# Forgetting attention and SwiGLU in one kernel: queries and keys of batch 0 loaded as two pairs of 256 tokens, with the written order redone

## Chip, cores and metric

The kernel runs on 1 core of one Trainium2 chip. The metric is device time in microseconds (us) of one execution; shorter is better.

## What is computed

The reference takes q, k, v of shape (8 batches, 8 heads, 576 tokens, 64) and a forget gate f, and feeds the attention's output, as 4608 rows of 512, to a SwiGLU layer of width 1536:

```
scores = scale * q @ k^T + (cum[:, None] - cum[None, :])     # cum = cumsum(log f), causal
attn   = softmax(scores);   x = attn @ v
xn     = x / sqrt(mean(x*x) + 1e-6) * rms_g
out    = (silu(xn @ w_gate) * (xn @ w_val)) @ w_out
```

## The kernel before, in words

Tokens of a batch are cut into five pieces j = 0 to 4 (four of 128 tokens, one of 64). For each batch, q and k are loaded from memory with a cast from float32 to bfloat16 by DMAs that POOL issues; each piece is turned so that the head dimension lies on the partitions; scores of a piece of queries against one piece of keys are one tile (8 small matmuls, `score_block`, L510); ACT takes the exponential (L552); POOL masks the diagonal tile (L560); PE multiplies with the scaled values (`values`, L566, matmuls in L581); DVE divides (L600, L604); `norm` (L613) makes the normalised rows, which PE turns for batches 0 and 1 (L651) and the DMA engines turn for the others. From there `gate` (L828) multiplies with w_gate and w_val (L838), and `project` (L877) with w_out (L916). The last token groups use a scheme with seven products for eight (`seven`, L746, matmuls in L773).

How a piece of q or k is loaded and turned:

- `load_qk` (L334) loads one piece of 128 tokens: one DMA for q and one for k (issued at L340). In memory one token of one head is a run of 256 bytes.
- `load_qk2` (L345) loads 256 tokens in one DMA (issued at L352). Partition p holds tokens 2p and 2p+1, so that one run is 512 bytes. Its buffers are four places of the tile `wt`, which is needed for weights only later; in the trace these DMAs and matmuls therefore carry the name `wt`.
- `turn_pe` (L448) turns a piece on PE for batches 0 and 1: 4 transposes for a single piece (L458), 16 for a pair (L464). One copy each then takes the turned q (DVE) and k (ACT) out of PSUM into QT and KT (L476).
- `PAIRS` (L16) says which pieces begin a pair. Before, batch 0 has a single piece 0, a pair of pieces 1 and 2, and a single piece 3 (loop at L413); batch 1 has two pairs.

The work is not ordered by a scheduler at run time. Every instruction group is a unit, made in a fixed order of creation by `P.add`; `Plan.run` (L125) then sorts the units by a written rank: each two letters of `ORDER` (L34) are the rank of one unit, in base 62, in order of creation. `SLOTS` (L75) gives in the same way the buffer that each use of a ring takes. Each engine works through its own units strictly in this order, and waits where an operand or a buffer is not there yet. PE has two score buffers (`sc`), so that a block of two score tiles needs the exponentials of the two tiles before it to be done. POOL's order holds its DMA issues, its masks and small steps of `norm`, one behind the other; SP issues the other DMAs. `load_w` (L369) loads thirds of w_gate and w_val (called wg0, wv0, wg1 and so on below).

Of the kernel before, what the change touches and what calls it, by code (L numbers as in the profile page):

```python
# [31 lines left out]
WEIGH_ACT = "gv"  # L32
LETTERS = string.digits + string.ascii_letters
ORDER = (  # L34
    "0302000105060y0C0g0b0h040l0i0m0p0q0z0c0d0F0M0K07080e0f090a0n0o0j0k0w0x0O0P0t0u0D0E0r0s14151p1q1y1z1U"
    "1V2f2g38392K2L3T3U0H0I0R0S1e1f1J1K18190Y0Z2y2z2V2W32333v3w2q2r3P3Q3H3I4a4b4w4x4B4C5j5k3A3B4f4g5X5Y4o"
    "4p4S4T5S5T4J4K6r6s71724Z506G6H7o7p6v6w7e7f8u8v6l6m6Q6R9s9t7G7H6A6B8j8k7L7M8e8f9M9N9q9r9Y9Za0a1ayazaN"
    "aO9w9x9D9E9Q9Rb4b5apaqaDaEbMbNbcbdcAcBbHbIcQcRc6c7egehcGcHcLcMf0f1bubvdsdtg4g5dfdgcZd0gagbdXdYezeAfo"
    "fpeFeGe3e4dhdidKdLg7g8hWhXesetfAfBgEgFgPgQgVgWiqirhbhchKhLhdheinioiQiRhshtjpjqiBiCkLkMh1h2iwixgJgKkl"
    "kmkgkhlhlikqkrkAkBkPkQlElFlllmmkml0v0A0B0G0N0J0Q0W0U0V0L0T17121a161k1u1h1m1o1r1v1E0X1b1d1g111B1H1N1S"  # L40
    "221Y231j1n1s1A252x2M272c2k2m24281F1Q3t2t2A2P2G2S2Y343r413i3s3m3z4n3Z443J3K4t4u3o4G5i5a4k4l4E4F6f5s5z"
    "5D5H5Q6b686c5w5x5o5p6g624P4Q5E5F786i6x6M6t5c5d5L5M7y6E6O6X6K747n7k7s63646S6T7T7x7I7B7S827Z8476777h7i"
    "8P8c8z8r7C7D7N7O9k8M8X8Z94969d7X7Y898a9U9h9p9l9L8n8o7t7uaI9C9H9O8T8U9A9Bbo9Wacaia8araHaLa6a7avawaSb2"
    "b8bhbfbUc2bXcdaXaYbrbsa9cbaeafamanbAcicncucvbabbbjbkdncDcPd6cKcWdpdcdRcEcFd2d3cUdGdPdWe6eledeNdvdwdI"
    "dJfveCePeKdkdle0e1gddHeWfbfNeZfHcycze8e9gwfiftfGgjf9fadSdTgIfUg3fXeHeIgegffZghgngpgogyh0gTfQfRglgmfS"
    "h9hjhBhghGi2icihejekhEhFjhhVhOhPgrgsjMipiEj4iyi0i1i6i7jGiLj3jyiSj9jgjmjTiuivieifhSjzjNjFjXksk0k8jCjD"
    "jKjLijkCkKkHk3k4kbkclNjnkTkYl1l0lWiYiZjVjWlzlblAlIm0kUkVkEkFmylOlYlTl9lalolpm9mamjmqmfmumDmImdmemEmF"
    "nkmPmTnsmWn7ncnand101i131c1w1x1D1G1M1R1T1Z2a2e2j2n2C2E2U36353a3c3f3L3S4h4q4M4W4Y5e5V656n6u6W6Z797g7m"
    "7v7A7F7R7V81888m8A8t8y9c9ia2a5ajatauaAaCaMb6bgbibnbGbLbRbVcJcOcVcYd1d5dqdAdNdQeqeyeJeOeYfff8fdgcgigq"
    "gugxgCgNgSgXgZhihlhyhAi8idiAiIjejljvjEjOjQjYk2k7kekkkpkzkIkWlcl7lfm6mimcmhmmmomrmCmzmHmJmNmVmYnJnNnX"  # L50
    "o3o7og1l1t1C1I1O1L1P1W1X21262b2i2o2w2u2F2R2Z31aTdzlnm4m53d3j3n3W4L4V3y3V405K5C5P61676d6j6I6L9b9yf7hw"
    "hx8g8b8l8W9f9g8E8J8K8w8C8G8R90918O9899bEeoeSeUeVb0aRb3bKbPbQblbybzbObZc3ccckclc9cfcgfLiJmpmvmwdEecee"
    "erewexeDfgfhfjfmfrfxfCfDfzfJfKhTjck5l3l4gHhphvhCiFiGhNiNiOikiXj1j6jajbj8jjjkkRltoqqYqZkokjkwl6lUlVld"
    "lwlxlglrlJn2n5n6m8mLmMmAmGojonoomtmZnznSoJoKpcpJpKo1oSoYp8pzpApmprpspupyqiqQqR202l292h2s2d2v2p2B2H2D"
    "2N2J2Q2X3k3E3q3x3N3D3M3R585W484z662I3p2O2T3C3u423F3X49303e3b3h3l373Y3g3G46434U4D4N534X4i5545524e4j57"
    "4c4y4v4A4H4r4R4I4O543O4m474d4s6C6o5q6h737a6V6F5b6a5n5r6p5A6e5R5Z6k7r7W7Q80836Y8B7d7l8H5u6z5O6N7b5g5G"
    "5t5y5J7c7E7w7z7P7K877U8d8i8q8L8I8Q958S97939e9o6P7j70757q8h8F8p8s8Nc0cec5cacj9Sa49Xaaad9Pab9T9VahaPaW"
    "aVb7beagaGalaoaKbmbJbtbBbScmcNcrcwcTakbqasaBbxbwbWbDbFc1c4cpchcocCbCc8bTbYcqaxaUaFaQaZfEg6fPg2ggcSde"
    "cXd7dof3flfefkfFdyebdMeaeieneMeveLf6d8dVdjdre2fMgYfVfYh4fcfIfqfyfOd4dmd9dddxeffseBeEfwgRhfh5h7hmdudO"
    "dBdFe5ibitiiiDiKgLh3gOgUh8iHj2iMiTj7h6hIhahhiahkhrhohqhDhnilhHi5izhzhYhMhRi4jBjPjJjUk6iPjoj0jdjAj5k1"  # L60
    "jujHkaigjiimisjrgtgDgzgGgMkvmUn0nGljlHocn8nwlCmQngmOnqnvnxnFnEnCnInQnRnUo6nZnAnOofomnTo4obovoioyoCoF"
    "nKnWo8oIoGoNoeoDn1ntnlnrnDk9lkkfktlvmKnhn4nbnukdkNkxkSl2mSnMnpnyo0lelKlulBlPlslSlDlLlZlGmnm3mbmxnLo9"
    "ounBpgpjptpCpnpEpMpPpRpWpTqbpBpYpXq1q8q9qcqhqoquqkqCpFqeqwqFqgqmqvqynHnPosoznVokotoMoOoVoQp4oaohoHp0"
    "olopoLp7oRp3papbnYorpfpioXpGpqpNo2o5oBp2odoAoEp9p1plpopppdpkpHpSpwpvpOqPpUq0r1q4oPpDpIq7pQr5pVq3qlqt"
    "r4qpqxqBqAqDqEqKqOqTr2rdqWrorerprsrvrwrzrDrRrJrSrVs0qSrOrys4rirZsgslq6qfqGqJqqqIqUqVr3rjr7rtqNr0qXrk"
    "r6rarfrqrmrFrurPqsrgrUrYrLs2rEs8rGrQs7serWs3s6sjsbsisusms5s9sascshsdsnsfsCsKsqsTsksxsLsWsOsSsFsXrxrA"
    "rKrIrTspsAsDsrstswsHszsGt2t6sEsMsNsUsQt0tht3tqtAtktIsItbt9tNtctnsRtEt8titytBtvtttxtYunusu1uKtMtXtStZ"
    "uhu4u7u6uputubuItPukuMuQuaueuuuwsYt1tdtgtatjtptltztFtstWtotuu2u5tGtOtTugu0u8uiudtmtJufumu3ulucuq515B"
    "5m7J595N5h6y565f5l5v9m9n5I5U60696q6D9J9K6J6U85868x8Dcsct8V9a929v8Y9z9Ga3dadb9u9F9j9IaJb1f4f5b9bpdCdD"
    "cxcIjsjtdUepemfndZe7eueRg0g1eTeXeQf2fufTgAgBgkgvjRjSfWg9iViWhuhUhJkihQhZi3i9jwjxiUjfjIjZknkym1m2kGkO"  # L70
    "owoxkukJnnnokDkXl5lqkZl8lylMlQlRlXm7mgmsmBmRninjmXn3nenfn9nmoToUoZp6peqaoWp5phpxuDuEpLq2pZq5qdqnr8r9"
    "qrqzrbrcqjqHqLqMrlrCrrsyrhrnrBrHrMrNrXs1sosssvsBtQtRsVsZt4t5sJsPtUtVt7tetwtDtftrtCtHtKtLujuouruxu9uy"
    "uBuCuGuVuXuYuzuJuNuOuAuFuHuTuvuPuUv0v3v4v1v2uLuSuRuWuZv6v9vavhvivbvlvpvqvnvovmvtvwvxvuvvv5v8vfvgvcvd"
    "v7vevjvkvrvs")
SLOTS = (  # L75
    "751b7a6362435110692802330754611170531262234023077651332432705b415542030169201a3302681541266b20177132"
    "2014533279005a6532661701135841742b721169332872410a23133054512665001739727a00200b42516118624543301b17"
    "71260040183951042a633112223573007b576333221173001561043122201100167312010541110321076100101454210733"
    "1011601200461031045720101103775012610544301702070101354106121015470017210034110611070104132015456013"
    "6100232017101455410630720011241100713104560011601234710070150277155011443103601200201571041750163132"  # L80
    "0101244100751104542016110324110701060053043233321311301053041033210111005004211241051100150340532013"
    "5310011221152001320353033202132013312230214131322301201202006220311303000143015262410033052722315103"
    "5261610735230212317213710230012635070323111010023111111000033110311200012110300131022003000032112100"
    "2201100120113110321031112300301010002101113003011020020102210220031010101011133102110101001311301103"
    "1102010311010122002100211001013200230113310131121103001211133012101200112100210020002171654506371011"
    "0103211330113002201331011012110026174342511114721231650015433657002001265345146210057101423570136474"
    "7252111003105406640115412730640007213167565012100433222217616210003112431260112012333003166262100310"
    "00004522412001200020465002100141510131034120020751351457312030266221127301205346576122415734323406")
# [981 lines left out]
```

## Time and profile before

| | us |
|---|---|
| median of 3 runs | 352.58 |
| lowest and highest run | 352.28, 355.83 |
| the profiled execution's own time | 351.74 |
| its span in the profile | 350.0 |

The span runs from the first to the last event that the profiler records; 1.74 us of the profiled execution lie around it. "Busy" is the time in which an engine has an instruction under way. Busy time of PE (TensorE's matmuls) includes the time until the last result of a group is out, so two groups that follow closely overlap a little in the listing. The DMA engines are a common resource of all queues.

### The profile page before, as it was taken

What the parts mean: (1) busy time and instruction counts of PE and PEld (TensorE: products, weight loads), DVE (VectorE), ACT (ScalarE), POOL (GpSimd) and SP (SyncE); (2) the same over time, 40 slices, a digit from 0 to 9 for tenths busy, and PEclk for the clock granted to TensorE, in tenths of its full rate; (3) what the DMA queues carried; (4) which work ended last, traced back from release to release, by engine and by line L of the source; (5) the groups of instructions that cost most, each with busy time, mean ns of one, the idle gap of its engine ahead of it and who ended that gap; (6) DMA issues with size and microseconds to landing.
All of it is one profiled execution on the core that took longest, in us unless ns stands there. A gap on an engine that the chain in (4) does not pass through costs nothing.

```text
span 350.0 us, 10530 instructions
## 1 busy us (share of the span) xinstructions
PE 333.9 (95%) x4289; PEld 259.9 (74%) x4314; DVE 275.3 (79%) x515; ACT 265.8 (76%) x440; POOL 204.5 (58%) x244
## 2 busy tenths in 40 slices
...
GB/s 128 215 217 233 200 153 137 155 149 117 182 136 162 162 157 147 198 140 165 182 174 122 180 168 139 166 84 121 3 85 45 2 76 62 2 30 36 59 90 153
DMA packets 159465, 44.89 MB, mean 128 GB/s; under 512 B 145012, under 2 KB 158840, under 8 KB 159416
## 3 DMA queue, kind: packets, MB, share of 16 engines
...
q14 instruction: 15, 0.12, 0.2%
...
## 4 chain that ended last, share of the span: by engine, by line
PE 87%; DVE 4%; ACT 2%; DMA 2%; issue 2%; POOL 1%; DVEq 0%; ACTq 0%; POOLq 0%
PE ff L838 31%; PE ff L916 19%; PE late L773 10%; PE ff L773 8%; PE sc L533 7%; PE ff L581 7%; PE late L916 4%; DMA qk<-in_q_dram 2%; ACT PT L552 1%; DVE ga L852 1%; PE ff L464 1%; POOL qk L340 1%; DVE KT L737 1%; POOL wt L352 0%; DVE x L604 0%
## 5 line engine op out<-in xcount | busy, mean ns | idle before, releaser
L552 ACT ACTIVATE PT<-sc 128x1024 bf16<-128x1024 f32 x96 | 94.7, 1023 | 20.0 <-PE sc L533 19.8
L838 PE MATMUL ff<-xT,wv 128*128 128x128 bf16 (+2 forms) x452 | 67.3, 289 | 1.6 <-DVE ga L852 1.1
L838 PE MATMUL ff<-xT,wg 128*128 128x128 bf16 (+2 forms) x451 | 67.5, 289 | 0.8
L845 DVE SCALAR_TENSOR_TENSOR hT<-ga,ff 128x512 bf16<-128x512 f32 x68 | 46.0, 684 | 14.3 <-PE ff L838 11.3
L824 POOL TENSOR_TENSOR hT<-PT,PT 128x512 bf16<-128x512 f32 x20 | 25.9, 1310 | 53.5 <-DVE PT L800 27.6
L852 DVE SCALAR_TENSOR_TENSOR ga<-th,ff 128x512 f32<-128x512 f32 x68 | 46.1, 682 | 9.2 <-ACT th L850 8.1
L850 ACT ACTIVATE th<-ff 128x512 f32<-128x512 f32 x68 | 40.0, 597 | 13.1 <-PE ff L838 7.9
L838 PEld LDWEIGHTS <-wv 128*128 128x128 bf16 x464 | 36.0, 98 | 18.2 <-issue 1.0
L838 PEld LDWEIGHTS <-wg 128*128 128x128 bf16 x464 | 35.9, 98 | 16.9 <-issue 0.2
L916 PEld LDWEIGHTS <-hT 128*128 128x128 bf16 x432 | 41.4, 98 | 6.8 <-issue 0.2
L560 POOL TENSOR_SCALAR_AFFINE_SELECT PT<-PT 128x1024 bf16<-128x1024 bf16 x32 | 36.6, 1147 | 12.3 <-ACT PT L552 12.2
L581 PEld LDWEIGHTS <-PT 128*128 128x128 bf16 (+1 forms) x896 | 32.0, 102 | 8.4 <-issue 1.6
L581 PE MATMUL ff<-Vs,PT 128*128 128x65 bf16 (+1 forms) x896 | 37.2, 196 | 0.0
L604 DVE TENSOR_TENSOR x<-ff,rden 128x256 f32<-128x256 f32 (+1 forms) x80 | 33.9, 424 | 3.2
L916 PE MATMUL ff<-wo,hT 128*128 128x256 bf16 x288 | 35.4, 273 | 0.0
L916 PEld LDWEIGHTS <-sm 128*128 128x128 bf16 x324 | 31.1, 98 | 5.3 <-issue 0.7
L493 POOL TENSOR_TENSOR Vs<-v,decT 128x512 bf16<-128x512 f32 (+1 forms) x30 | 31.6, 1055 | 5.3 <-DMA v<-in_v_dram 5.2
L533 PE MATMUL sc<-QT,KT 64*128 64x128 bf16 (+1 forms) x960 | 33.6, 215 | 0.5 <-ACT PT L552 0.3
L533 PEld LDWEIGHTS <-KT 64*128 64x128 bf16 x960 | 24.6, 97 | 12.2 <-issue 10.8
L926 DVE TENSOR_TENSOR ores<-ores,ff 128x512 f32<-128x512 f32 (+1 forms) x38 | 25.2, 663 | 8.6 <-PE ff L916 7.9
L340 POOL DMA_DIRECT2D qk<-in_q_dram x34 | 29.9, 881 | 1.0 <-POOLq L1054 0.8
L340 POOL DMA_DIRECT2D qk<-in_k_dram x34 | 29.7, 875 | 0.0
...
## 6 DMA issues: line engine op xcount, KB each, us to landing
out_dram<-ores SPq DMA_DIRECT2D x32, 256.0 KB, 2.6
v<-in_v_dram SPq DMA_DIRECT2D x25, 256.0 KB, 4.3
qk<-in_q_dram POOLq DMA_DIRECT2D x26, 128.0 KB, 5.7
qk<-in_k_dram POOLq DMA_DIRECT2D x26, 128.0 KB, 5.9
v<-in_v_dram POOLq DMA_DIRECT2D x7, 256.0 KB, 7.3
wg<-in_moe_w_gate_dram POOLq DMA_DIRECT2D x3, 512.0 KB, 8.7
wv<-in_moe_w_val_dram POOLq DMA_DIRECT2D x3, 512.0 KB, 9.4
...
```

Source lines behind the costliest of these rows:

```text
L340: nc.gpsimd.dma_start(out=T_qk[h.slot][0:n, :].rearrange("p (h d) -> p h d", d=D), in_=src[b, :, p0:p0 + n, :].rearrange("h p d -> p h d"))
L533: nc.tensor.matmul(t[:, par, c:c + n], lhsT=kt[r, p, kj * 128:(kj + 1) * 128], rhs=qt[r, p, qi * 128:qi * 128 + n], start=not x, stop=True ...
L552: nc.scalar.activation(T_of_p[hp.slot][:, 0:2 * half].rearrange("p (a c) -> p a c", a=2)[:, :, 0:cols], T_sc[h.slot][:, :, 0:cols], ACT.Ex ...
L560: nc.gpsimd.affine_select(out=d, in_=d, pattern=[[0, 8], [1, n]], compare_op=ALU.is_ge, fill=0.0, base=0, channel_multiplier=-1)
L581: nc.tensor.matmul(T_ff[hpo.slot][r0:r0 + n, p * 65:p * 65 + 65], lhsT=T_of_p[h.slot][:, c:c + n], rhs=vs[:, kj, 2 * p + par, :], start=(k ...
L604: nc.vector.tensor_tensor(d, po[r0:r0 + n, :, 0:D], bcast(r[r0:r0 + n, :], D), ALU.mult)
L773: nc.tensor.matmul(t[:, c * HTK:(c + 1) * HTK], lhsT=w[:, d, (2 * u + c) * 128:(2 * u + c + 1) * 128], rhs=r[:, d, :], start=(start and c ...
L838: nc.tensor.matmul(T_ff[h.slot][:, c:c + n], lhsT=w[:, dc, fc * 128:(fc + 1) * 128], rhs=xT[:, dc, t0:t0 + n], start=(dc == 0), stop=(dc = ...
L845: nc.vector.scalar_tensor_tensor(hT, in0=three[0], scalar=0.5, in1=three[1], op0=ALU.mult, op1=ALU.mult)
L850: th = act(0.6, key - 0.1, lambda: nc.scalar.activation(T_th[ht.slot], T_ff[hg.slot], ACT.Tanh, scale=0.5), [ug], take=[ht])
L852: a = dve(0.69, key - 0.1, lambda: nc.vector.scalar_tensor_tensor(T_ga[ha.slot], in0=T_th[ht.slot], scalar=1.0, in1=T_ff[hg.slot], op0=ALU ...
L916: nc.tensor.matmul(t[:, s * HD:(s + 1) * HD], lhsT=a()[:, fc, s * 128:(s + 1) * 128], rhs=w[:, fc, :], start=(not more and s == ss[0] and ...
```

## The change

q and k of pieces 0 to 3 of batch 0 come as two pairs (pieces 0 and 1, pieces 2 and 3) instead of a single piece, a pair and a single piece. The strings for the order and the slots are replaced as a whole.

```diff
-PAIRS = {(0, 1), (1, 0), (1, 2)}
+PAIRS = {(0, 0), (0, 2), (1, 0), (1, 2)}
...
 ORDER = (
-    "0302000105060y0C0g0b0h040l0i0m0p0q0z0c0d0F0M0K07080e0f090a0n0o0j0k0w0x0O0P0t0u0D0E0r0s14151p1q1y1z1U"
+    "0302000105060l0y0j0m04070p0g0k0q0r0z0c0d0H180N08090e0f0a0b0n0o0h0i0s0t0B0C0u0v191a0w0x1o1p1H1I2f2g2P"
...
 SLOTS = (
-    "751b7a6362435110692802330754611170531262234023077651332432705b415542030169201a3302681541266b20177132"
+    "751372636241503001231174166372620321504021597b331a08526526416731330379225042501b0a137754001873414661"
...
-    for at, (j, two) in ((-16, (0, False)), (-15, (1, True)), (-13, (3, False))):
+    for at, (j, two) in ((-16, (0, True)), (-13, (2, True))):
         (load_qk2 if two else load_qk)(0, j, at)
         for i in range(j, j + 1 + two):
             load_v(0, i, at + 0.01)
```

There are 1956 units before and 1948 after: two loads fewer are made (an issue and a landing each) and two turns fewer (the transposes and their copy each). Read against the order of creation, the two `ORDER` strings begin like this on the engines. Here "q0" is q of piece 0, "q01" the pair of pieces 0 and 1, "b1" stands for batch 1, S(q,k) is a score tile of batch 0, V(q) the products with the values, "mask" POOL's mask of the diagonal tile of that query piece, T(j) the transposes of normalised piece j, G(j) the first products of `gate` for piece j:

```
POOL before  q0 k0 k12 q12 v3 q3 v1 k3 b1q01 v2 b1k01 mask0 b1k23 wg0 b1q23 b1v0 mask1 wv0 norm0 wg1 mask2 ...
POOL after   q01 k01 q23 v1 k23 v3 wv0 v2 b1q01 b1k01 b1q23 mask0 b1k23 mask1 wg0 b1v1 norm0 wg1 mask2 ...

PE before    turn q0, turn k0, decay, S(0,0), turn k12, turn q12, turn q3, V(0), S(1,0..1), V(0), turn k3,
             S(2,0..1), turn b1q01, S(2,2), turn b1k01, V(1), S(3,0..1), V(1), turn b1k23, T(0), V(2), S(3,2..3),
             V(2), T(1), G(0), turn b1q23, S(b1), V(3), ...
PE after     turn q01, turn k01, decay, S(0,0), turn q23, S(1,0..1), turn k23, V(0), V(0), S(2,0..1), V(1), V(1),
             S(2,2), S(3,0..1), turn b1q01, turn b1k01, S(3,2..3), V(2), T(0), V(2), T(1), turn b1k23, turn b1q23,
             S(b1), G(0), V(3), ...

ACT before   copy k0, exp(0,0), copy k12, exp(1,*) x2, copy k3, exp(2,*) x3, copy b1k01, exp(3,*) x2, copy b1k23, ...
ACT after    copy k01, exp(0,0), exp(1,*) x2, copy k23, exp(2,*) x3, exp(3,*) x2, copy b1k01, exp(3,*) x2, ...
```

Further on the same units come in another interleaving all the way; the end of PE's order (the products of the last group and four halves) is alike.

## Rows read from the trace of the kernel before

**Rows 1.** The page, part 1: busy time, share of the span, instructions

```profile
PE 333.9 (95%) x4289; PEld 259.9 (74%) x4314; DVE 275.3 (79%) x515; ACT 265.8 (76%) x440; POOL 204.5 (58%) x244
```

**Rows 2.** Busy by stretch: length, PE, PEld, DVE, ACT, POOL, granted clock, DMA share, GB/s

```profile
0.00:24.34 24.34, 15.81 (x239) 12.22 (x240) 19.18 (x53) 17.44 (x20) 21.65 (x30) 1.00 1.43 185
24.34:50.00 25.66, 25.47 (x516) 24.23 (x514) 24.11 (x47) 24.54 (x40) 20.10 (x29) 1.00 1.31 198
...
215.00:230.00 15.00, 13.78 (x188) 9.23 (x191) 13.47 (x21) 12.85 (x22) 10.60 (x12) 1.00 1.33 166
...
340.00:350.00 10.00, 5.09 (x46) 4.16 (x43) 3.60 (x8) 0.59 (x1) 0.00 (x0) 0.93 0.46 133
```

**Rows 3.** Timeline of PE: start, duration, instruction, idle before it

```profile
12.07 0.61 PE L458 MATMUL ff<-ident,qk 128*128 128x128 bf16 x4 [0.73 <-DMA qk<-in_q_dram]
...
15.89 0.61 PE L533 MATMUL sc<-QT,KT 64*128 64x128 bf16 x8 [0.30 <-ACT PT L552]
...
17.97 1.07 PE L464 MATMUL ff<-ident,wt 128*64 128x128 bf16 x16
...
19.52 1.04 PE L533 MATMUL sc<-QT,KT 64*128 64x128 bf16 x16
...
21.02 0.64 PE L464 MATMUL ff<-ident,wt 128*64 128x128 bf16 x16
...
24.34 1.06 PE L838 MATMUL ff<-xT,wg 128*128 128x128 bf16 x16
25.32 0.64 PE L464 MATMUL ff<-ident,wt 128*64 128x128 bf16 x16
...
26.45 0.66 PE L581 MATMUL ff<-Vs,PT 128*128 128x65 bf16 x16
...
226.90 0.81 PE L838 MATMUL ff<-xT,wv 128*128 128x512 bf16 x3 [1.07 <-DVE ga L852]
```

**Rows 4.** Timeline of ACT, copies and exponentials of the start

```profile
10.36 1.31 ACT L476 COPY KT<-ff 128x1024 bf16<-128x1024 bf16 x1
13.90 1.94 ACT L552 ACTIVATE PT<-sc 128x1024 bf16<-128x1024 f32 x2 [2.23 <-PE sc L533]
15.73 0.59 ACT L476 COPY KT<-ff 128x512 bf16<-128x512 bf16 x1
```

**Rows 5.** Timeline of POOL: issues of q0, k12, b1k23, wg0, b1q23, wv0; one mask

```profile
1.31 1.10 POOL L340 DMA_DIRECT2D qk<-in_q_dram  x1 [0.81 <-POOLq L1054]
...
3.29 0.90 POOL L352 DMA_DIRECT2D wt<-in_k_dram  x1
...
11.21 1.20 POOL L560 TENSOR_SCALAR_AFFINE_SELECT PT<-PT 128x1024 bf16<-128x1024 bf16 x1
12.26 0.99 POOL L352 DMA_DIRECT2D wt<-in_k_dram  x1
13.16 0.85 POOL L373 DMA_DIRECT2D wg<-in_moe_w_gate_dram  x1
13.90 0.99 POOL L352 DMA_DIRECT2D wt<-in_q_dram  x1
...
16.70 0.88 POOL L373 DMA_DIRECT2D wv<-in_moe_w_val_dram  x1
```

**Rows 6.** The same six issues, one each: KB written, us from issue to landing

```profile
qk<-in_q_dram POOLq DMA_DIRECT2D x1, 128.0 KB, 4.3
wt<-in_k_dram POOLq DMA_DIRECT2D x1, 256.0 KB, 5.4
wt<-in_k_dram POOLq DMA_DIRECT2D x1, 256.0 KB, 6.4
wg<-in_moe_w_gate_dram POOLq DMA_DIRECT2D x1, 512.0 KB, 8.6
wt<-in_q_dram POOLq DMA_DIRECT2D x1, 256.0 KB, 9.3
wv<-in_moe_w_val_dram POOLq DMA_DIRECT2D x1, 512.0 KB, 9.7
```

More of the change, by code (lines that the diff above doesn't have):

```diff
@@ L34 @@
 ORDER = (
-    "0302000105060y0C0g0b0h040l0i0m0p0q0z0c0d0F0M0K07080e0f090a0n0o0j0k0w0x0O0P0t0u0D0E0r0s14151p1q1y1z1U"
[L36 to L74, printed above, removed]
-SLOTS = (
-    "751b7a6362435110692802330754611170531262234023077651332432705b415542030169201a3302681541266b20177132"
[L77 to L88, printed above, removed]
@@ new lines @@
+    "0302000105060l0y0j0m04070p0g0k0q0r0z0c0d0H180N08090e0f0a0b0n0o0h0i0s0t0B0C0u0v191a0w0x1o1p1H1I2f2g2P"
+    "2Q1X1Y35360E0F0J0K1A1B1g1h0R0S0Y0Z2C2D292a2Y2Z2l2m494a2U2V3j3k4L4M3Q3R3K3L54553C3D4Z505R5S4d4e5f5g63"
+    "6457584R4S5K5L5z5A6j6k7b7c7k7l3Z406W6X6M6N7E7F6s6t797a7J7K9i9j7A7B8u8v9J9K8m8na9aa9V9W9A9Ba5a67W7X9F"
+    "9Gadaeapaqb0b1aVaWaLaMb6b7cPcQcsctdidjdYdZcNcObubvcucvd8d9cCcDaNaOcIcJd0d1evewdPdQdCdDfhfigegfdddefN"
+    "fOgBgCfxfyf7f8f3f4g5g6dRdSfYfZgvgwhdheh8h9ieifiYiZioipgXgYi8i9iHiIhyhzhjhkjKjLi2i3hKhLjxjyktkukokpkJ"
@@ new lines @@
+    "kKkykzkfkglBlClGlHljlkmUmV0A0D0G0I0L0M0P0V0Q0U110X140O0T0W151t161i1d1k1n1s1m1r1v1z1E1Q1K1R1u1x1w1D2y"
+    "2p231W2d2s271T1Z1P1U472o2u2J2z2G2N2T3c3q333p3O41484w4D3H3I3T3U5M4W535c42434l4m5Q5o5q5t5G5U61676b4T4U"
+    "4y4z6n6h4H4I5u5v736f6v6D6q5a5b5V5W7q6F6P6V6Z7d7o7j7u68695C5D6Q7y7L7P7U8b80876x6y71728e8q8y8O81826H6I"
+    "8S928W93969a9g7h7i8i8j9U9k9r9q9O898a9o9pa19H9Na38I8J9Q9RaAagamatarazaFaP9y9zaDaEaHb2b5babcbjbBbobAav"
+    "awaRaS9m9xaiajbYbZbFbTc3c9cfbQbRbKbLcgcFcLdpcYdadodhdKcyczdkdld6dBe2dJe9epeeekdHdIeOePfdeFeMfcdwdxd2"
@@ new lines @@
+    "d3eIeSfkfpfrfvfHezeAdUdVfBfFfJfPfWemenfTfUgbg1gcgseteugRgSh4gDgJgMgVh7hlhtgjgkh0h1iShQhThYhZi7ihimiO"
+    "g3g4fLfMfSgrgFgGgtguhFisizj5iPhphqiuiviFj1jljIj8jtjBjwjCiUiVjrjskPjJjUjOk3kck7kIjDjEjQjRl2klkAkvjajb"
+    "k0k1kCkkkLl4lqkTlsk8k9j2j3kWl8lplflWkRkSldlem0lKlYlQlllmlulvmsm3mdmjm8mkmqmumemflTlUnbmEmWn0mKn1n9n6"
+    "nk101712131b1f1e1j1G1L1M1V222c2h2k2F2M3237383e3f3m4i4o4B4F4Q4X51596c6g6B6K6R6Y74777r7v7M7Q7Z858d8k8o"
+    "8r8x8A9d9D9u9P9E9LaoauayaBaCaIb4bebwbCbGbJbNbXcmcxcUcXdLdTdXe7e3e6edeqeEeHeLeUfAfGg7gdgggigngEgAgIhm"
```

36 lines of the change are left out of this document (added).

## The prediction

> **What bounds the kernel now.** I read the page's busy shares first, then busy time by stretch, then the timelines of PE, ACT and POOL in the start, and last the landings of single DMAs. PE is busy for 333.91 of 350.0 us [rows 1, 2], so only 16.1 us can be won by better cover. The stretches say where they lie: 24.34 - 15.81 = 8.53 us before the first product of `gate`, 0.19 us from there to 50, 1.22 us between 215 and 230, and 10 - 5.09 = 4.91 us in the last 10 us, where the last results are added and stored [rows 2]. The other stretches share 16.1 - 14.85 = 1.24 us. From 24.34 us on PE has next to no gap, so whatever the change does to the moment at which PE is first kept full comes out at the end one for one, and that is where I look. The tail has the same last products and I take it as unchanged.
>
> The moment must be compared for equal work. After the change PE's order puts turn b1q23 and a score block S(b1) ahead of G(0); before, they come behind it. Before, G(0), the turn and the block are all done at 26.45, and G(0) itself takes 25.32 - 24.34 = 0.98 [rows 3]. So "as early as before" means for the new order: G(0) starts at 26.45 - 0.98 = 25.47.
>
> **The change, part by part.** *Work of PE, DVE, ACT, POOL.* Four turns of a single piece go, two turns of a pair come. A single turn's row is 0.61 us, but the next group starts 0.40 later; a pair's is 1.07 [rows 3]. That is 2 x 1.07 - 4 x 0.40 = +0.54 at most and 2 x 1.07 - 4 x 0.61 = -0.30 at least. I don't add it separately: the chain below holds every turn. ACT copies two pairs instead of two singles and a pair: 1.31 - 2 x 0.59 = +0.13 [rows 4]; it stands in the chain too. POOL makes two issues fewer, some 0.9 each [rows 5], -1.8 us, and gains nothing by it while the DMA queue is the slower part, as the next point shows.
>
> *The first landings.* Counting float32 as it is read, q0, k0 and k12 are 256 + 256 + 512 KB, and k12 lands at 3.29 + 5.4 = 8.69 [rows 5, 6]. The new q01 and k01 are the same 1024 KB, issued at the same first places, so k01 lands at 8.69 by that row. By the pace of the following stretch it could be earlier: from 8.69 to the landing of b1k23 at 12.26 + 6.4 = 18.66 come 3328 KB, 0.77 us per 256 KB, against 3.08/3 = 1.03 between q0 (1.31 + 4.3 = 5.61) and k12; with 0.77 it is 5.61 + 3 x 0.77 = 7.9. I take 8.4, near the row of the same transfers.
>
> *The score chain.* From k01: turn 1.07 (9.5), copy of the pair on ACT 1.31 (10.8), the block S(0,0) of 8 matmuls 0.61 (11.4), its exponential 1.94/2 = 0.97 (12.4). Meanwhile turn q23 (11.4 to 12.4), then S(1,0..1), 1.04 (13.5), two exponentials 1.94 (15.4), copy k23 1.31 (16.7), three exponentials of piece 2 (19.6). Only then is the second score buffer free for S(3,0..1), which ends at about 20.0. Before, the same block ended at 19.52 + 0.97 = 20.49 [rows 3, 4]. On scores the new order is thus 0.5 us ahead. But PE's fillers are gone from that stretch: before, three of the four turns of batch 1 lay between these blocks or right behind, after, all four come behind S(3,0..1).
>
> *From there to G(0).* Left at 20.0 are 4 turns of pairs, 2 score blocks, V(2) twice (12 matmuls each), T(0) and T(1). PE shows two paces for the same form: 16 transposes take 1.07 at 17.97 and 0.64 at 21.02 [rows 3], though the granted clock reads 1.00 (2.4 GHz) in the whole stretch [rows 2]. By net times (start to start) of the quick pace, 0.57 a turn, 0.55 a block, 0.46 and 0.3 the others, the list is 4 x 0.57 + 2 x 0.55 + 2 x 0.46 + 2 x 0.3 = 4.9 us, 24.9, and some 0.3 more since S(3,2..3) waits for two exponentials: 25.2. (0.46 and 0.3 are estimates, by the ratio of the matmul counts to the block's 16.) By the slow pace each is about 1.8 times that, 8.7 us: 28.7.
>
> *The weights.* wg0 moves on POOL from 13.16 to behind mask1, and wv0 ahead of batch 1. By the time b1q23 landed before, 13.90 + 9.3 = 23.2, batch 0's q, k, v, all four pairs of batch 1 and one third of a weight had come in [rows 5, 6]. The new queue has just these ahead of wg0 (with wv0 as the third), so the last of them lands at 23.2 again. wg0 itself took 13.16 + 8.6 - 18.66 = 3.1 us; by wv0, at 16.70 + 9.7 = 26.4 and with one v between, (26.4 - 23.2) x 1024/1280 = 2.6 us. So wg0 lands between 25.8 and 26.3, against 21.76 before, where PE came for it only at 24.34. On POOL the added waits are these: after eleven issues (11.2, where mask0 starts before too [rows 5]) mask0 now waits for its exponential until 12.4, and mask1 for its own until 14.4; behind them stand the issues of b1k23 and wg0. A mask takes 1.2 and an issue 0.9, so wg0 is issued around 15.7, while the DMA queue has work until 23.2: nobody waits for it. SP's first issues keep their order. I take 26.3, by the same transfer's own row. G(0) can start neither before this nor before PE has come there.
>
> *What is late next.* wg1 is next, one v (0.8) and 3.1 us behind wg0: 30.2. PE wants it after some 5.4 us of products behind G(0), at 31.7, so 1.5 us of cover are left. The other engines' work in that stretch is the same.
>
> *The rest of the order.* Everything is interleaved anew, with the same instructions. The remaining gaps of 0.19 + 1.22 + 1.24 = 2.65 us can go, at best -2.65; at worst new waits come. The longest wait of PE there now is 1.07, for a buffer that DVE frees [rows 3]; I bound the loss by three such, +3.2, and take 0.
>
> **The sum.** G(0) at 26.3 against 25.47: +0.8. That is 351.74 + 0.8 = 352.5 for an execution like the profiled one; the median shown lies 0.84 above that execution, so 353.4 us is the forecast, no difference that a measurement can tell (about 1% of 352.58, 3.5 us, can be told from no change).
>
> **The pace of PE, read with the skill.** The trace: PE worked without a gap from 15.89 on and the 16 transposes went from 1.07 to 0.64 some 5 us later [rows 3]. The Trainium skill (TensorE: Matmul & The Clock Gate, Part 1: The HAM clock gate) says that the engine's default is half rate and that sustained activity releases it; by that rule the durations agree and the granted clock's column does not show it. It speaks against a change that opens gaps in the start. What it would make of the time is rival 2.
>
> **The rivals.**
> 1. *The longer runs make batch 0 quicker.* Reading 512 bytes instead of 256 per run could halve the time of the four single pieces, 4 x 1.03/2 = 2.1 us of the queue. Then wg0 lands at 24.2, k01 some 0.7 earlier, and PE comes to G(0) at 24.5: -1.0, 351.6 us. For it: the start waits for DMA (q0 lands at 5.61 [rows 5, 6], and PE waits 0.73 at 12.07 [rows 3]). Against it: in the rows the weights, with longer runs still, take 3.1 us per 1024 KB, the same 0.77 per 256 KB as the mix of pieces. The Trainium skill (DMA: Bandwidth & Descriptors, Specifications) puts line rate at 512 bytes and more, which would favour this rival; the rows just named don't.
> 2. *PE stays at the slow pace* (the slower side). Place: from 20 to 27 us. With gaps before S(3,0..1) the quick pace would come some 5 us after 20.0, as it did after 15.89: at 25.0 slow work of 5.0 us is done, the other 3.7 take 2.1, G(0) starts at 27.1: +1.6, 354.2 us; wholly slow +3.2, 355.8. It decides from the point at which PE's chain ends later than wg0's landing, 26.3. For it: the two waits behind the exponentials of piece 2. Against it: the chain keeps PE busy nearly without a gap from 10.8 to 17.
> 3. *The new order opens waits later.* Three more like the one at 226.90 on top of the forecast: 353.4 + 3.2 = 356.6 us. For it: ACT has 24.54 of 25.66 us busy and DVE 24.11 just behind the start [rows 2], so a unit that slips finds little slack. Against it: the work per stretch is alike.
> 4. *It closes the waits that are left*, all 2.65 us: 350.8 us. For it: the 1.07 is one spot. Against it: all of them at once is unlikely.
>
> **How the numbers follow.** Forecast 0.50, rival 1 0.12, rival 2 0.18, rival 3 0.10, rival 4 0.10. The range runs from rival 4 (350.7) to just short of rival 3 (356.4); it leaves out about a fifth: most of rival 3, the ends of rival 4 and sums of two. Faster by over 1% (under 349.1) would need rivals 1 and 4 together and more: 0.03. Slower by over 1% (over 356.1) is rival 3, and rival 2 at its end: 0.11. Within 1%: 0.86.
>
> **What would show it.** Right, if in the new profile k01's turn starts near 8.4, S(3,0..1) ends near 20, G(0) starts between 25.8 and 26.8 with wg0 landing just before, and PE has about 9.3 us idle before it for the same work. The pace is read from the 16 transposes of batch 1: 0.64 for the forecast, 1.07 for rival 2. Rival 1 shows as wg0 landing near 24. The forecast is wrong if PE's gaps behind 27 us differ from 2.65 by more than 1 us, or if the first product comes before 25.

## The result, and the profile after

The changed kernel takes 358.03 us (median of 354.87, 356.04, 360.02 and 360.18) against 352.63 for the kernel before beside it: 1.0132 times, interval [1.0087, 1.0177]. That is slower, outside the range of 350.7 to 356.4. The runs lie in two groups, near 355 and near 360, and the second section says why. (The ratios here leave out runs more than 1.5% above the fastest of the same kernel, which takes much of an upper group out of them; so the runs are named beside them.) The profiled execution is one of the lower group: 356.04, span 354.3, as before 1.74 more than its span. Against 351.74 it has lost 4.30 us. (In the rows PE is TensorE's matmuls, DVE VectorE, ACT ScalarE, POOL GpSimd and SP SyncE.)

Busy time of the changed kernel by the stretches of [rows 2] (same columns):

```profile
0.00:24.34 24.34, 13.93 (x222) 11.29 (x223) 16.74 (x48) 16.14 (x17) 19.67 (x27) 0.87 1.33 184
24.34:50.00 25.66, 25.66 (x524) 24.61 (x522) 23.11 (x45) 24.89 (x41) 21.81 (x29) 0.99 1.38 202
...
100.00:215.00 115.00, 109.68 (x1294) 68.28 (x1308) 86.28 (x161) 84.36 (x136) 79.91 (x100) 1.00 1.40 152
215.00:230.00 15.00, 14.49 (x190) 10.00 (x190) 14.05 (x23) 12.72 (x22) 11.32 (x10) 1.00 1.68 175
...
340.00:354.30 14.30, 9.99 (x90) 8.54 (x88) 8.69 (x14) 0.59 (x1) 0.57 (x1) 0.94 0.48 140
```

One row of the kernel before that its groups do not have, the long stretch in the middle:

```profile
100.00:215.00 115.00, 113.97 (x1359) 71.13 (x1375) 86.30 (x167) 88.13 (x144) 85.98 (x104) 1.00 1.50 161
```

Read the second number of each row against the first. PE's idle time grew by 15.81 - 13.93 = 1.88 us in the first stretch and by 113.97 - 109.68 = 4.29 between 100 and 215. It shrank by 0.19 up to 50, by 14.49 - 13.78 = 0.71 between 215 and 230, and by 4.91 - 4.31 = 0.60 in the tail. That makes +4.67; PE's own work is 0.37 shorter (333.54 against 333.91), which leaves the 4.30. So the start, on which the forecast rested, is the smaller part, and the larger lies where the forecast put nothing.

PE's timeline of the changed kernel: the points of the start that the prediction named, then the waits of the middle:

```profile
8.97 1.07 PE L463 MATMUL ff<-ident,wt 128*64 128x128 bf16 x16 [0.70 <-DMA wt<-in_k_dram]
...
11.42 0.61 PE L532 MATMUL sc<-QT,KT 64*128 64x128 bf16 x8 [0.47 <-ACT KT L475]
...
19.94 0.61 PE L532 MATMUL sc<-QT,KT 64*128 64x128 bf16 x8 [0.31 <-ACT PT L551]
20.48 1.92 PE L463 MATMUL ff<-ident,wt 128*64 128x128 bf16 x32
...
26.85 1.07 PE L837 MATMUL ff<-xT,wg 128*128 128x128 bf16 x16
...
161.91 0.52 PE L532 MATMUL sc<-QT,KT 64*128 64x64 bf16 x16 [0.61 <-DMA KT<-qk]
...
172.19 1.02 PE L837 MATMUL ff<-xT,wg 128*128 128x512 bf16 x4 [1.80 <-DMA xT<-xn]
...
204.22 1.02 PE L837 MATMUL ff<-xT,wg 128*128 128x512 bf16 x3 [1.67 <-DVE ores L925]
...
218.27 1.47 PE L915 MATMUL ff<-wo,sm 128*128 128x256 bf16 x12 [0.35 <-DVE ores L925]
```

The bracket of the last four rows is the wait and what ended it. Three of them, 0.61, 1.80 and 1.67, are most of the 4.29. The first two end with transposes that the DMA engines make (KT and xT). The one at 204 is put down to an addition (`ores`, the function `plus` of `project`) that frees a PSUM bank. VectorE shows why that addition is late:

```profile
199.95 3.62 DVE L899 TENSOR_TENSOR sm<-hT,sm 128x1536 bf16<-128x1536 bf16 x1
203.49 0.68 DVE L925 TENSOR_TENSOR ores<-ores,ff 128x512 f32<-128x512 f32 x1
...
215.85 1.77 DVE L890 TENSOR_TENSOR sm<-hT 128x1536 bf16<-128x1536 bf16 x1
```

The sum ahead of it took 3.62 us. In the kernel before, most sums of this form (128x1536, both operands in SBUF) take 0.95 or 0.96. The longest takes 1.84, and there two masks of GpSimd run beside it:

```profile
224.41 1.84 DVE L737 TENSOR_TENSOR KT<-QT,wv 128x1536 bf16<-128x1536 bf16 x1
```
```profile
224.17 3.03 POOL L560 TENSOR_SCALAR_AFFINE_SELECT PT<-PT 128x1024 bf16<-128x1024 bf16 x2
```

GpSimd's timeline in the changed kernel, at the moment of the 3.62:

```profile
199.05 0.65 POOL L559 TENSOR_SCALAR_AFFINE_SELECT P<-P 128x512 bf16<-128x512 bf16 x1
199.68 1.03 POOL L492 TENSOR_TENSOR Vs<-v,decT 64x512 bf16<-64x512 f32 x1
200.66 0.97 POOL L339 DMA_DIRECT2D qk<-in_k_dram  x1
201.65 1.10 POOL L559 TENSOR_SCALAR_AFFINE_SELECT PT<-PT 128x1024 bf16<-128x1024 bf16 x1
```

GpSimd runs without a break until 201.65 + 1.10 = 202.75, and the sum ends 0.82 later, at 203.57: as if it had stood still until GpSimd was through and then run. This was the theory to test, beside the rival that the start's lateness shifts everything behind it.

### The profile page after: what moved, and what is told of

Its sections match the earlier page's. It is cut to its first block, busy times and chain, and to the rows that moved or that the text cites. A ratio compares the mean times of both kernels' runs of the same rounds, so it can differ in the third digit from the quotient of the medians.

```text
span 354.3 us, 10566 instructions
## 1 busy us (share of the span) xinstructions
PE 333.5 (94%) x4304; PEld 261.2 (74%) x4330; DVE 276.5 (78%) x514; ACT 265.5 (75%) x439; POOL 205.3 (58%) x242
## 4 chain that ended last, share of the span: by engine, by line
PE 84%; DMA 5%; DVE 2%; issue 2%; SPq 2%; ACT 2%; POOL 0%; DVEq 0%; POOLq 0%
PE ff L837 30%; PE ff L915 16%; PE ff L772 9%; PE late L772 8%; PE sc L532 7%; PE ff L580 7%; PE late L915 5%; DMA xT<-xn 2%; DMA wt<-in_k_dram 2%; PE ff L463 1%; DMA KT<-qk 1%; ACT PT L551 1%; SPq L442 1%; SPq L664 1%; ACT KT L475 1%
## 5 line engine op out<-in xcount | busy, mean ns | idle before, releaser
L837 PE MATMUL ff<-xT,wv 128*128 128x128 bf16 (+2 forms) x452 | 68.1, 289 | 0.7 <-DVE ga L851 0.2
L559 POOL TENSOR_SCALAR_AFFINE_SELECT PT<-PT 128x1024 bf16<-128x1024 bf16 x32 | 37.8, 1182 | 35.4 <-ACT PT L551 35.0
L580 PEld LDWEIGHTS <-PT 128*128 128x128 bf16 (+1 forms) x896 | 32.2, 102 | 10.4 <-POOL PT L559 1.7
L492 POOL TENSOR_TENSOR Vs<-v,decT 128x512 bf16<-128x512 f32 (+1 forms) x30 | 33.6, 1125 | 2.4 <-DMA v<-in_v_dram 2.2
L915 PE MATMUL ff<-wo,hT 128*128 128x256 bf16 x252 | 30.9, 273 | 0.0
L925 DVE TENSOR_TENSOR ores<-ores,ff 128x512 f32<-128x512 f32 (+1 forms) x36 | 23.7, 660 | 8.2 <-PE ff L915 7.9
L642 ACT ACTIVATE xn<-x,rs 128x512 bf16<-128x512 f32 (+1 forms) x38 | 27.1, 721 | 3.0 <-POOL rs L634 3.0
L339 POOL DMA_DIRECT2D qk<-in_k_dram x32 | 27.7, 868 | 0.1
```

The costliest lines, as they stand in the source:

```text
L492: eng.tensor_tensor(T_Vs[hv.slot][0:n, j, :, 0:D], T_v32[h.slot][0:n, :, :], bcast(dj, D), ALU.mult)
L559: nc.gpsimd.affine_select(out=d, in_=d, pattern=[[0, 8], [1, n]], compare_op=ALU.is_ge, fill=0.0, base=0, channel_multiplier=-1)
L580: nc.tensor.matmul(T_ff[hpo.slot][r0:r0 + n, p * 65:p * 65 + 65], lhsT=T_of_p[h.slot][:, c:c + n], rhs=vs[:, kj, 2 * p + par, :], start=(k ...
L837: nc.tensor.matmul(T_ff[h.slot][:, c:c + n], lhsT=w[:, dc, fc * 128:(fc + 1) * 128], rhs=xT[:, dc, t0:t0 + n], start=(dc == 0), stop=(dc = ...
L915: nc.tensor.matmul(t[:, s * HD:(s + 1) * HD], lhsT=a()[:, fc, s * 128:(s + 1) * 128], rhs=w[:, fc, :], start=(not more and s == ss[0] and ...
```

## The experiments

**Which half of the order costs?** Two kernels with the two orders crossed at some 85 us. The first has the changed loads and the changed order up to its 586th unit, then the units that are left in the order of the kernel before. The second has the loads and the order of before for 594 units and the changed order behind them.

```diff
-ORDER = (all units as changed)
+ORDER = (586 units as changed, the others as before)     # new_start_old_rest
+ORDER = (594 units as before, the others as changed)     # old_start_new_rest
```

> The changed kernel's loads and order up to about 85 us, the order before from there on. Theory 'order' (the start costs about 1.4 us, the interleaving behind 100 us the rest): slower than before by 1 to 2 us, 353.6 to 354.6, with PE idle between 100 and 215 us near 1.0. Rival 'start' (the late start itself sets the later waits off, whatever the order): slower than before by 3 to 6 us, with several us of PE idle between 100 and 215 us.

> The loads and the order before up to about 85 us, the changed kernel's order from there on. Theory 'order': slower than before by 2 to 5 us, and PE idle between 100 and 215 us of 3 us or more. Rival 'start': within 1 us of before, PE idle there near 1.

Measured: new start, old rest 352.37 us (351.84 to 353.23, 12 runs), 0.9996 [0.9982, 1.001]; old start, new rest 360.23 us (358.27 to 365.09, 5 runs), 1.0193 [1.0162, 1.0223]. The pairs and the redone start cost nothing that can be measured, not even the 1 to 2 us that I expected, so the loss comes from the redone order behind 85 us. How it is made up there the second kernel does not tell. It loses 7.7 us, more than the 2 to 5 expected and more than the change itself. Of its profile's waits one is also the changed kernel's: 1.68 us at 207.02, behind a sum of 3.63. Others are its own: 2.36 at 116.74 for a mask of GpSimd and 0.72 at 112.18 for a scaling, some 30 us behind the crossing. The profiles of the changed kernel and of the kernel before have no wait there.

**The pair buffers and the pace of PE in the start.** In the changed kernel two issues of GpSimd wait for places of the pair buffer (0.89 us at 10.34, 2.12 at 13.33), and PE falls back to half pace. One kernel gives the pairs seven places for four (three in the part of `wo` that is loaded later); one puts ten blocks of four extra matmuls into PE's gaps between 14 and 20 us.

```diff
-    sizes = dict(qk2=4, ...
+    sizes = dict(qk2=7, ...
```
```diff
-WARM = {}
+WARM = {(0, 0): 5, (0, 1): 5}
```

> The changed kernel with seven places for pairs instead of four (three more in the half of the tile wo that is loaded last), so that POOL's issues of batch 1's pairs no longer wait for PE (0.89 and 2.12 us before the change of places). Theory 'DMA queue' (the queue has work all the time): the first product of gate stays within 0.4 us of 26.85 and the time within 1 us of the changed kernel. Rival 'buffer': the landings of batch 1 and of wg0 come 2 us earlier and the first product by 1 to 2 us.

> The changed kernel with ten blocks of four extra matmuls of the identity on PE, put before four waits between 15 and 19 us; their results are not used. Theory 'pace' (the granted clock fell to 0.50 at 18 us because PE was idle for a third of 15 to 19 us): the granted clock stays at 1.00 there, the 16 transposes of batch 1 take 0.64 instead of about 1.0, and the first product starts where wg0 lands, about 26.0 instead of 26.85. Rival 'no pace': the clock falls all the same, or the product does not move.

Measured: more_pair_buffers 358.68 us (355.19, 356.51, 356.59, 360.77, 361.11, 361.14), 1.0096 [1.0064, 1.0127]; pace_fillers 361.11 (359.43 to 363.25, 6 runs), 1.0248 [1.0218, 1.0278]. Neither helps: G(0) starts at 26.36 and 26.56, 0.49 and 0.29 earlier than 26.85, and the time does not come down. With the extra matmuls the granted clock does stay at 1.00 up to 50 us, and the 32 transposes of batch 1 at 20.98 take 1.08 us for 1.92; that half of the theory 'pace' held, but G(0) still came behind PE's own chain and not at 26.0. What the second shows is the upper group of times. Its VectorE, GpSimd and PE around 215 us:

```profile
213.86 5.79 DVE L892 TENSOR_TENSOR sm<-hT 128x1536 bf16<-128x1536 bf16 x1
219.58 0.68 DVE L927 TENSOR_TENSOR ores<-ores,ff 128x512 f32<-128x512 f32 x1
```
```profile
213.73 1.08 POOL L494 TENSOR_TENSOR Vs<-v,decT 128x512 bf16<-128x512 f32 x1
214.73 1.11 POOL L561 TENSOR_SCALAR_AFFINE_SELECT PT<-PT 128x1024 bf16<-128x1024 bf16 x1
215.78 3.04 POOL L494 TENSOR_TENSOR Vs<-v,decT 128x512 bf16<-128x512 f32 x3
```
```profile
220.31 2.08 PE L917 MATMUL ff<-wo,sm 128*128 128x256 bf16 x9 [4.37 <-DVE ores L927]
```

The same sum that took 1.77 us in the changed kernel's profile (at 215.85) took 5.79 here, and PE waited 4.37 where it had waited 0.35. The profile of more_pair_buffers, an execution of 360.77, has the same two numbers, 5.79 and 4.37. GpSimd's run ends at 215.78 + 3.04 = 218.82 and the sum 0.83 later. The difference of the two waits, 4.0 us, is most of the 4.6 us between the two groups of runs. Behind the wait PE was slow for a while as well: its next 12 matmuls took 2.72 us where the changed kernel's took 1.47, and the granted clock read 0.50 (1.2 GHz) from 220.3 to 222.0.

**The sums behind what they held up.** The two sums change places with what stood behind them on VectorE; nothing else moves.

```diff
 ga (g=4)
-fourth sum of g=3
 ores += ff (g=3)
 hT (g=4), 1/den and x (batch 5, last piece)
+fourth sum of g=3
...
-first sum of g=4
 ores += ff (g=3), ga (g=5), 1/den and x (batch 6)
+first sum of g=4
 second sum of g=4
```

> The changed kernel with two units moved in VectorE's order alone: the fourth sum of the blocks of hT of g=3 and the first of g=4 (128x1536 each, the two that took 3.62 us and, in the runs near 360 us, 5.79 us) stand behind the additions to ores and the divisions of the output of attention that they held up. Theory, that TensorE stands still behind these two long sums because the addition behind them frees its PSUM bank late: the waits at 204 (1.67 us) and 220 (0.35 or 4.37 us) go, the wait of 1.80 at 172 stays, and the time is 353.5 to 355.0, with a spread under 1 us in place of 354.9 to 360.2, since the 4 us between the two kinds of run are the second wait. Rival, that the sums are long for another cause and hold up whatever is behind them: then the wait moves to the gates or the sums of the next stage and the time stays at 355.5 to 360.

Measured: 353.81 us (353.40 to 356.25, 12 runs), 1.0048 [1.0027, 1.0068]. The upper group is gone, and so are the waits at 204 and 220. (The spread, 2.85, is wider than the 1 us expected: two of the twelve runs lie at 355.81 and 356.25.) Both sums are short now:

```profile
202.35 0.96 DVE L899 TENSOR_TENSOR sm<-hT,sm 128x1536 bf16<-128x1536 bf16 x1
...
215.36 0.95 DVE L890 TENSOR_TENSOR sm<-hT 128x1536 bf16<-128x1536 bf16 x1
```

In this execution GpSimd stood idle beside both, from 201.33 to 206.83 and from 212.58 to 217.24, so the run shows what the two waits cost and not yet why the sums were long. One part of the expectation failed, the 1.80 at 172 that was to stay: PE waits 0.41 for xT at 170.78, not 1.80, and has a wait of 1.34 for xT at 136.04 and one of 1.12 for KT at 220.16 instead. The waits for the DMA-made transposes (xT, KT) stand in other places in each profile. But they go with the new order: all eight profiles with the new order behind 85 us have one to three of them, 0.26 to 1.80 us each, and none of the six with the old order there has any. In the profile of sums_behind they are all of PE's waits of 0.25 us or more behind 26 us. No run took all of them away.

**The turns of xT.** SyncE's queue in the changed kernel:

```profile
159.89 1.25 SPq L664 DMA_TRANSPOSE xT<-xn  x1
161.24 0.55 SPq L362 DMA_DIRECT2D v<-in_v_dram  x1
161.88 4.29 SPq L664 DMA_TRANSPOSE xT<-xn  x3
```

The four turns of batch 4 stand around a load of v, and the last one, issued at 164.95, landed 7.0 us later, when PE had waited 1.80.

```diff
 SP   turn xT (tokens 128 to 255)
-SP   load v (batch 6, piece 0)
+SP   turn xT (tokens 0 to 127)
 SP   turn xT (tokens 256 to 383), turn xT (tokens 384 to 511)
-SP   turn xT (tokens 0 to 127)
+SP   load v (batch 6, piece 0)
```

ScalarE's multiplication that makes the normalised rows of tokens 0 to 127 moves ahead with their turn.

> The changed kernel with the normalized rows of (batch 4, tokens 0 to 127) multiplied behind those of tokens 128 to 255 on ScalarE and turned by SyncE ahead of the other two tiles of that batch, and the load of v of (6, 0) on SyncE's queue behind all four turns rather than ahead of three. Theory, that the wait of 1.80 us at 172 is the last of these turns, issued at 164.95 and landed 7.0 us later behind the loads: the last turn is issued near 163.6 and the wait falls to 0.4 or less; the median falls by 1.4 to 1.8 and the two kinds of run stay: 353.3 to 354.8 or 358 to 359. Rival, that the turns are slow because of the loads of q and k on GpSimd's queue: the last turn lands as late as before, wait 1.2 to 1.8.

Measured: 354.26 and 354.47 in two runs, 359.38 to 360.94 in nine. The wait at 172 is gone (no wait for xT behind 26 us is left in the profile), the 1.67 stays, and the two groups stay, as expected. The lower group is at 354.3 to 354.5 where the changed kernel's is at 354.9 and 356.0, and the upper group is not lower; the fall of the median by 1.4 to 1.8 did not come. So this wait was worth less than its 1.80.

**GpSimd works but reads nothing.** The order stays as changed; for batches 5 to 7 GpSimd writes a constant where it scaled v or masked P.

```diff
+            if b >= 5 and eng is nc.gpsimd:
+                eng.memset(T_Vs[hv.slot][0:n, j, :, 0:D], 0.5)
+                return
             eng.tensor_tensor(T_Vs[hv.slot][0:n, j, :, 0:D], T_v32[h.slot][0:n, :, :], bcast(dj, D), ALU.mult)
...
+                    if b >= 5:
+                        nc.gpsimd.memset(d, 0.5)
+                        return
                     nc.gpsimd.affine_select(out=d, in_=d, pattern=[[0, 8], [1, n]], compare_op=ALU.is_ge,
```

> The changed kernel with its order as it is, where GpSimd's work of batches 5 to 7 is replaced: the scaling of v by the decay (Vs) and the masks on P write a constant and read nothing. This leaves the scaling and the masks of these batches out. Theory, that VectorE's sum of two operands in SBUF stands still while GpSimd's instructions that read SBUF run back to back: every sum of 128x1536 behind 150 us takes 0.95 to 1.05, the waits at 204 and 220 go, and the time is 353.5 to 355.0 in every run. Rival, that any work of GpSimd beside the sum lengthens it, or its DMA issues do: the sum at 200 stays at 2 us or more (the DMA issue of 0.97 stands in the middle of its 3.62).

Measured: 353.73 us (352.77 to 357.26, 10 runs), 1.0053 [1.0024, 1.0082]. The waits at 204 and 220 behind a long sum are gone. Three runs, at 355.96, 357.14 and 357.26, lie above the 355.0 expected for all, and the one profile, of 354.24, does not show why. The sums that took 3.62 and 1.77 or 5.79, on VectorE, and GpSimd beside them:

```profile
199.03 0.95 DVE L905 TENSOR_TENSOR sm<-hT,sm 128x1536 bf16<-128x1536 bf16 x1
...
213.20 0.95 DVE L896 TENSOR_TENSOR sm<-hT 128x1536 bf16<-128x1536 bf16 x1
```
```profile
198.51 0.95 POOL L339 DMA_DIRECT2D qk<-in_k_dram  x1
199.46 0.98 POOL L563 MEMSET PT<- 128x1024 bf16 x1
...
212.72 0.57 POOL L493 MEMSET Vs<- 128x512 bf16 x1
213.31 0.95 POOL L563 MEMSET PT<- 128x1024 bf16 x1
```

All twelve sums between 158 and 228 take 0.95 or 0.96, beside writes and beside a DMA issue; the one at 213.20 has writes beside it for nearly all of its length. So it is GpSimd's reading that holds the sum, not its being at work. This is the strongest evidence of the study, since no instruction of VectorE or PE was moved. The Trainium skill (SBUF — State Buffer, Who interferes with whom) says so too: an instruction of VectorE with two inputs in SBUF contends with one of GpSimd that reads SBUF, not with one that only writes.

**Both edits at once.**

> Both edits in the changed kernel: the two sums behind what they held up, the turns of batch 4 early. Theory, that these three waits (1.80, 1.67, 0.35 or 4.37) are the loss behind 85 us: 351.7 to 353.3, level with the kernel before (ratio 0.998 to 1.003). Rival, that the new order has lost slack everywhere, so that the next wait opens as one is closed: 354 or more.

Measured: 353.41 us (352.26 to 356.00, 12 runs), 1.0034 [1.0011, 1.0057], just above the band expected and well below the rival's. Of the 1.3% some 0.3% are left: its profile shows a wait of 1.51 us for KT at 218.95 and one of 0.73 at 160.84, others than those closed; the first is once more a wait for a transpose by DMA.

**The same edit where nobody changed anything.** The kernel before has a wait of 1.07 us at 226.90 [rows 3]. There too a sum stands ahead: the second sum of the value weights (L737), 1.84 us beside two masks. It is moved behind ga and hT, once in the kernel before and once with the new start and the old rest.

```diff
-KT <- QT - wv (second sum of the value weights)
 ga, hT (g=5)
+KT <- QT - wv (second sum of the value weights)
```

> The kernel before (single pieces, its own order) with one unit moved in VectorE's order: the second sum of the value weights (128x1536, 1.84 us at 224.41 beside two masks of GpSimd) stands behind ga and hT of the gates that it held up. Theory, that the wait of 1.07 us at 226.90 is the same thing as the waits of the new order (an addition late behind a long sum): it goes, and the time is 351.2 to 351.7, ratio 0.996 to 0.9985. Rival, that the wait was tanh late on ScalarE or moves to the next gate: 352.3 to 352.8.

> The changed kernel's pairs and its order up to 85 us, the order of the kernel before behind that, and the same sum moved. Theory, that the start with pairs is level with the old one within 0.3 us and the wait of 1.08 at 227.65 goes: 351.0 to 351.7, ratio 0.995 to 0.998, and within 0.4 of the run above. Rival, that the start costs the 0.8 us of the prediction: 352.0 or more, 0.6 to 1.0 above the run above.

Measured: 351.40 us (350.56 to 353.73, 12 runs), 0.997 [0.9948, 0.9993], and 350.88 us (350.40 to 351.48, 12 runs), 0.9951 [0.9932, 0.9971]. The wait is gone in both, and both beat the kernel before by about what it was worth. VectorE in the second one:

```profile
225.54 0.67 DVE L851 SCALAR_TENSOR_TENSOR ga<-th,ff 128x512 f32<-128x512 f32 x1
226.43 0.69 DVE L844 SCALAR_TENSOR_TENSOR hT<-ga,ff 128x512 bf16<-128x512 f32 x1 [0.21 <-PE ff L837]
227.04 1.39 DVE L736 TENSOR_TENSOR KT<-QT,wv 128x1536 bf16<-128x1536 bf16 x1
```

ga is done at 226.2, not behind the sum, and the sum is still long (1.39) but nobody waits for it. The second kernel is the fastest of the study: the pairs are no loss, given an order that does not put sums in the way. Whether they gain by themselves is open, since the intervals of the two overlap.

**How long is a sum held?** In the kernel before, GpSimd gets extra work beside the sums of the last groups, where it was idle: 1, 2, 4 and 6 scalings back to back.

```diff
+BESIDE = {5: 1, 6: 2, 7: 4, 8: 6}
...
+                for i in range(BESIDE[g]):
+                    nc.gpsimd.tensor_tensor(T_Vs[0][:, 0, :, 0:D], T_v32[0], bcast(decT[:, 0, 0:H], D), ALU.mult)
```

> The kernel before with work added on GpSimd alone: behind the first sum of the blocks of hT of the groups 5, 6, 7 and 8, GpSimd runs 1, 2, 4 and 6 scalings of v (1.05 us each, the form of Vs) into a place that nothing reads any more; the sums that follow on VectorE took 0.95 us there. Theory, that a sum which comes while GpSimd's readings run back to back is held for the whole run: the second sum takes up to 1.6 in group 5, up to 2.7 in group 6, 3 to 4.8 in group 7 and 5 to 7 in group 8, wherever GpSimd was first. Rival, that it gets its turn behind the one that is running: 1.0 to 2.0 whatever the number. The time rises by 0 to 5 us, by what TensorE waits for there.

Measured, the run of six on GpSimd and the sums on VectorE:

```profile
334.73 8.44 POOL L906 TENSOR_TENSOR Vs<-v,decT 128x512 bf16<-128x512 f32 x6
```
```profile
334.80 1.78 DVE L892 TENSOR_TENSOR sm<-hT 128x1536 bf16<-128x1536 bf16 x1
336.62 1.68 DVE L895 TENSOR_TENSOR hT<-hT 128x1536 bf16<-128x1536 bf16 x1
338.22 1.79 DVE L898 TENSOR_TENSOR sm<-sm,hT 128x1536 bf16<-128x1536 bf16 x1
...
342.25 1.72 DVE L901 TENSOR_TENSOR sm<-hT,sm 128x1536 bf16<-128x1536 bf16 x1
```

My theory of a whole run fell. Here a sum waits for one scaling, takes its turn, and the next scaling waits for the sum: the first four scalings start at 334.73, 335.85, 337.56 and 339.28, and the six take 8.44 us, where six of 1.05 would take 6.3. No sum beside the scalings took more than 1.81, whatever their number. The time is 354.82 us, 1.0074 [1.0044, 1.0104].

A last run puts a DMA issue and masks among the scalings; in group 8 two DMA issues, a scaling, a mask and two scalings, as at 213.7.

```diff
-BESIDE = {5: 1, 6: 2, 7: 4, 8: 6}
+BESIDE = {5: "dvvv", 6: "dvvvv", 7: "vdm", 8: "ddvmvv"}
```

> As the run with readers beside the sums, with other work in the same places on GpSimd: in group 5 a DMA issue and three scalings, in group 6 a DMA issue and four scalings, in group 7 a scaling, a DMA issue and a mask (the sequence of the sum that took 3.62 us), in group 8 two DMA issues, a scaling, a mask and two scalings (the sequence of the sum that took 5.79). The run before showed 1.07 to 1.81 us whatever the number of scalings, which fell with the theory that the sum waits for the whole run. Theory now, that a DMA issue of GpSimd ahead of or among its readers keeps the run closed to the sum: at least one sum of groups 6 to 8 takes 2.5 us or more. Rival, that it is the place and not the DMA issue: all sums stay at 0.95 to 1.9, and what kept the sum out for 3.62 and 5.79 us stays open. Time not looked at: it holds the added work.

Measured in one run (356.40 us, with the added work in it), GpSimd and VectorE in group 8:

```profile
341.44 0.88 POOL L907 DMA_DIRECT2D v<-in_v_dram  x1 [4.08 <-DMA v<-in_v_dram]
342.34 1.06 POOL L913 TENSOR_TENSOR Vs<-v,decT 128x512 bf16<-128x512 f32 x1
343.33 1.10 POOL L910 TENSOR_SCALAR_AFFINE_SELECT Vs<-Vs 128x1024 bf16<-128x1024 bf16 x1
344.39 2.77 POOL L913 TENSOR_TENSOR Vs<-v,decT 128x512 bf16<-128x512 f32 x2
```
```profile
342.11 4.15 DVE L901 TENSOR_TENSOR sm<-hT,sm 128x1536 bf16<-128x1536 bf16 x1
```

The long hold is back: the sum, ready at 342.11 while GpSimd only issued a DMA, let a scaling, a mask and a scaling pass and took its turn between the last two scalings. In group 6, behind a DMA issue but among scalings alone, the sums took 1.63 and 1.68; in group 7, with a scaling, a DMA issue and a mask as at 199.68, 1.08 and 1.47. So a mixed run can shut a sum out for several instructions. Whether the DMA issue right before it or the change between scaling and mask does that stays open, and two other sums speak against either alone. In the profile of sums_behind a sum took 2.29 at 224.06: it waited for one mask and was passed by a second, behind a DMA issue and with no scaling between them. The sum at 215.85 in the changed kernel also came right behind DMA issues, and took 1.77, one turn.

## Why the prediction was wrong

**What failed is "the rest of the order", taken as 0 and bounded by three waits like the one at 226.90, +3.2.** The idle time between 50 and 340 grew by 4.29 - 0.71 = 3.6 us in an execution of the lower group and by some 4 us more in the upper one. Of the waits that make up the 3.6, 1.67 stands behind a sum that GpSimd held, and 0.61 and 1.80 are for transposes by DMA, with which my bound did not reckon at all. Rival 3 named the mechanism (new waits, VectorE without slack) and got 0.10; its size was off. I took the longest wait that the old order happened to have as the price of a wait. But 1.07 is what the same hold costs when the sum loses 0.89 us (1.84 for 0.95); it can lose 2.7 (3.62) or 4.8 (5.79), and then the wait is 1.67 or 4.37. The rows to ask were on VectorE, which I did not read there: sums of one form, 0.95 or 0.96 in most places and 1.33 to 1.84 in five. Where one form has several durations, it is worth asking who worked beside it, for the order decides that.

**The start, term by term.** The first landing: k01 at 2.41 + 6.5 = 8.9, not 8.4 and beyond the bound of 8.69. The score chain held: S(0,0) at 11.42 for 11.4, S(3,0..1) ending at 20.5 for 20.0. wg0 was issued at 17.29, not 15.7, since the issues of batch 1 waited for places of the pair buffer, which I had not seen; it landed at 17.29 + 8.7 = 26.0, inside 25.8 to 26.3, because the DMA queue had work, as said. G(0) came at 26.85 for 26.3, behind PE's own chain and not behind wg0. So the term of +0.8 was 26.85 - 25.47 = +1.4 in this execution, and PE was idle for 10.4 us before G(0), not 9.3. In the eight other profiles of the start with pairs G(0) came between 25.66 and 26.57, around the forecast.

**+0.8 at the end one for one** did not show: the new start with the old rest is 0.1 us below the kernel before, not 0.8 above. Two profiles that differ in the start alone, both with the weight sum moved, show part of why: before 26 us PE is idle for 9.61 us in the new start and 9.29 in the old one, between 26 and 50 for 0.00 against 0.27, and its work is 0.35 shorter. That the rest is the noise of single profiles is argued, not shown.

**The tail** was not quite unchanged: 4.31 us idle for 4.91.

**Rival 1** (longer runs quicker) fell: k01 landed 0.2 us later than k12 did, and wg0 near 26, not 24. **Rival 2** (PE at slow pace) came true in the profiled execution at about its price: PE did two turns in 1.92 us at 20.48 and was quick again only from 25; G(0) at 26.85 where that rival said 27.1. But it is not the loss: extra work in the gaps kept PE quick and brought G(0) forward by 0.29 and no shorter time, and with the same slow turns (1.92 at 20.22) new start and old rest is level with before. **Rival 4** was right in one thing: the wait of 1.07 could be closed, for about 1 us, by an edit that the change did not make.

By the prediction's own test, PE's gaps behind 27 us within 1 us of 2.65, the forecast was wrong, by 3 us and more.
